# Hashed attention into a gated feed-forward: score and value matmuls in groups of six key tiles instead of three, and bit masks as second tensors

## Chip, cores and metric

The kernel runs on one core of a Trainium2 chip. The metric is device time in microseconds (us), the median of the runs shown, lower is better. A profile is one execution, recorded instruction by instruction; its times are from the start of its span.

## What is computed

Attention over 4 batches, 8 heads, 768 positions and a head width of 64, in which a query sees only the keys of its own hash bucket; then two matrix products with x * sigmoid(1.702 x) between.

```python
q_bits = (np.einsum('bhsd,dk->bhsk', q, proj) > 0).astype(np.int64)
k_bits = (np.einsum('bhsd,dk->bhsk', k, proj) > 0).astype(np.int64)
q_bucket = np.sum(q_bits * powers, axis=-1)          # six bits
k_bucket = np.sum(k_bits * powers, axis=-1)
mask = q_bucket[:, :, :, None] == k_bucket[:, :, None, :]
scores = np.where(mask, scale * np.matmul(q, k.transpose(0, 1, 3, 2)), -1000000000.0)
attn = np.exp(scores - np.max(scores, axis=-1, keepdims=True))
attn = attn / (np.sum(attn, axis=-1, keepdims=True) + 1e-09)
x = np.matmul(attn, v)                               # (B,H,S,D) -> (B*S, H*D) = 3072 x 512
h = x @ w_in                                         # 512 x 2048
return (h * (1.0 / (1.0 + np.exp(-1.702 * h)))) @ w_out
```

The weights arrive as float64 and are turned into float32 on the chip, by operations on their bits.

## The kernel before

**Stages.** Attention fills the first 345 us and leaves its result, transposed, in `xT`. The feed-forward stage (from line 632 on) does both products with seven block products in place of eight. It is not touched by the change but for its share of the weight conversion.

**Pairs, halves and groups.** The attention loop goes over 16 pairs of heads. The two heads of a pair lie on the two halves of the 128 partitions. Each pair has two halves c of its 384 queries, and six key tiles of 128. The loop before works in groups of three key tiles (GT = 3), so a pair is four groups. For a group:

- `scores` (L368, L369): for each key tile two matmuls of bf16 hash features, which add a large negative number where the buckets differ, and the float32 scores, as two 64-row matmuls side by side, into one of three PSUM buffers (`sps`, two banks each). ScalarE takes the exponential of a buffer into the tile `es[c]`; there is one `es` for each half.
- `add`: the sum over key tiles, for the denominators. GpSimd adds the first three tiles (L378, L379) into `acc0`, of which there is one buffer. VectorE adds the other three and `acc0` (L382 to L384).
- `values` (L392): matmuls of the exponentials with v, which accumulate all six tiles into `av`.
- `unload` (L403, L404): ScalarE copies `av` to `xT`.
- `total` (L410): the denominators as a matmul `dn` of the sum with ones. `invert` (L417, L419): VectorE transposes `dn` out of PSUM and takes the reciprocal. `norm` (L424, L425): VectorE transposes back and multiplies `xT`.

**The next pair** is prepared meanwhile: `turn` (L329, VectorE transposes k and q), `measure` (L336, ScalarE, sums of squares), `hashed` (L346, matmuls `hash`), `featured` (L351 on VectorE, then eight DMAs, L356, on the SP queue), `fetch` and `fetch_v` (DMAs of k, q and v, L291 and L298, on SP).

**PSUM.** The eight banks are taken: six by the three score buffers, one by `av`, one by the pool `mps`, of one buffer, in which `dn` of every half and `hash` of every pair take turns.

**Weight conversion** (`convert`, from L141). One chunk of 128 x 512 numbers for each of the pairs 1 to 14, in steps that `step` calls between other work: the DMA of `raw`; sign and bits (L155, L156); exclusive or (L158); a mask (L161) and, on ScalarE, the square for a size test (L163); a multiply of the low words (L165); an add (L167); and a multiply by the size test (L170). The remaining 18 chunks are converted in the feed-forward stage.

**Order.** TensorE, VectorE, ScalarE and GpSimd take their instructions in the order in which the program writes them (`manual_schedule`). A scheduler places only the DMAs of the SP queue. So an instruction that waits holds all that is written behind it on its engine. At group g the loop writes: scores of g; invert of a half finished earlier; turn and measure; norm; add, values and unload for group g - 1; hashed, featured and fetches; total of the half that ended at g - 3; conversion steps.

Of the kernel before, what the change touches and what calls it, by code (L numbers as in the profile page):

```python
# [8 lines left out]
F32 = mybir.dt.float32  # L9
# [10 lines left out]
P = 128  # L20
# [18 lines left out]
def kernel(  # L39
# [98 lines left out]

    CW = 512

    def convert(cv, dst, src, queue=nc.sync):  # L141

        raw = cv.tile([P, CW, 2], U32, tag="raw", name="raw")
        queue.dma_start(out=raw, in_=src)

        def of(x):
            return x if len(dst.shape) == 2 else x.rearrange("p (j d) -> p j d", j=dst.shape[1])

        lo, hi = raw[:, :, 0], raw[:, :, 1]
# [5 lines left out]
        nc.vector.tensor_scalar(sign, hi, 0x80000000, 0x40000000, op0=Alu.bitwise_and, op1=Alu.bitwise_or)  # L155
        nc.vector.tensor_scalar(bits, hi, 3, 0x7FFFFFFF, op0=Alu.logical_shift_left, op1=Alu.bitwise_and)  # L156
        yield
        nc.vector.tensor_tensor(bits, bits, sign, op=Alu.bitwise_xor)  # L158
        yield

        nc.vector.tensor_scalar(sign, bits, 0xFF800000, None, op0=Alu.bitwise_and)  # L161

        nc.scalar.activation(size, hi.bitcast(F32), Act.Square)  # L163
# [90 lines left out]
    def attention(ff):  # L254
# [4 lines left out]
        with actx:  # L259
# [99 lines left out]
            def scores(n, c, kts):  # L359
                qT, kT, qf, kf = xts[n, "q"], xts[n, "k"], feats[n % 2]["q"], feats[n % 2]["k"]  # L360
                cols = slice(c * HS, (c + 1) * HS)
                for kt in kts:
                    ps = sps.tile([P, 2, 512], F32, tag="s", name="ps")
                    keys = slice(kt * P, (kt + 1) * P)
                    for a, m, last in ((kf, qf, False), (kT, qT, True)):
                        for j in range(2):
                            hs = slice(D * j, D * (j + 1))
                            nc.tensor.matmul(ps[:, j, 0:HS], a[hs, keys], m[hs, cols], start=not last, stop=last)  # L368
                    nc.scalar.activation(es[c][:, kt, :, 0:HS], ps[:, :, 0:HS], Act.Exp, scale=1.0 / D**0.5)  # L369

            accs, avs = {}, {}

            def add(n, c, kt):

                e = [es[c][:, kt + i, :, 0:HS] for i in range(3)]
                if kt == 0:
                    acc = accs[n, c, 0] = st.tile([P, 2, HS], F32, tag="acc0", name="acc0", bufs=1)
                    nc.gpsimd.tensor_tensor(acc, e[0], e[1], op=Alu.add)  # L378
                    nc.gpsimd.tensor_tensor(acc, acc, e[2], op=Alu.add)  # L379
                else:  # L380
                    acc = accs[n, c] = st.tile([P, 2, HS], F32, tag="acc", name="acc")
                    nc.vector.scalar_tensor_tensor(acc, e[0], T * TINY, e[1], op0=Alu.add, op1=Alu.add)  # L382
                    nc.vector.tensor_tensor(acc, acc, e[2], op=Alu.add)  # L383
                    nc.vector.tensor_tensor(acc, acc, accs.pop((n, c, 0)), op=Alu.add)  # L384

            def values(n, c, kt):
                if kt == 0:
                    avs[n, c] = aps.tile([P, HS + 1], F32, tag="av", name="av")
                av, vt = avs[n, c], vts[n]
                for t in range(kt, kt + GT):  # L390
                    for j in range(2):
                        nc.tensor.matmul(av[D * j : D * (j + 1), :], vt[:, t, j, :], es[c][:, t, j, :],  # L392
                                         start=(t == 0), stop=(t == T - 1))
# [6 lines left out]
            def unload(n, c):  # L400
                av = avs.pop((n, c))
                vs = st.tile([P, 1], F32, tag="vs", name="vs")
                nc.scalar.copy(vs, av[:, HS : HS + 1])  # L403
                nc.scalar.activation(x_of(n, c), av[:, 0:HS], Act.Identity, bias=vs[:, 0:1])  # L404
# [7 lines left out]
            def invert(n, c):  # L412


                dn = accs.pop((n, c))
                rt = st.tile([P, HS], F32, tag="rt", name="rt", bufs=1)
                nc.vector.transpose(rt, dn)  # L417
                r = st.tile([P, HS // 32, 1], F32, tag="r", name="r")
                nc.vector.reciprocal(r, rt.rearrange("p (s i) -> p s i", i=32)[:, :, 0:1])  # L419
                accs[n, c] = rt, r  # L420

            def norm(n, c):
                rt, r = accs.pop((n, c))
                nc.vector.transpose(rt.rearrange("p (s i) -> p s i", i=32), r.to_broadcast([P, HS // 32, 32]))  # L424
                nc.vector.tensor_tensor(x_of(n, c), x_of(n, c), rt, op=Alu.mult)  # L425

            groups = [(n, c, kt) for n in range(len(pairs)) for c in range(2) for kt in range(0, T, GT)]
            last = len(pairs) - 1
            conv = {}

            def step(n, count=1):
                for _ in range(count):
                    next(conv.get(n, iter(())), None)
# [18 lines left out]
            started = {}  # L452
            first_pair()
            fetch_v(0)
            for x in "kq":
                fetch(1, x)
            for g in range(len(groups) + 4):
                n, c, kt = groups[g] if g < len(groups) else (last + 1, 0, 0)
                at = 2 * c + kt // GT
                if n <= last:  # L460
                    scores(n, c, range(kt, kt + GT))

                turns = at - (n == 0)
                if g in started:
                    invert(*started[g])
                if n < last and 0 <= turns < 2:
                    turn(n + 1, "kq"[turns])
                    measure(n + 1, "kq"[turns])
                if g in started:
                    norm(*started.pop(g))  # L470
                if 1 <= g <= len(groups):
                    add(*groups[g - 1])
                    values(*groups[g - 1])
                    if groups[g - 1][2]:
                        unload(*groups[g - 1][:2])
                if n < last and turns == 1:
                    hashed(n + 1)
                    featured(n + 1)
                    for x in "kq":
                        if n + 2 <= last:  # L480
                            fetch(n + 2, x)
                    fetch_v(n + 1)
                if 3 <= g <= len(groups) + 2 and groups[g - 3][2]:
                    total(*groups[g - 3][:2])
                    started[g + 1] = groups[g - 3][:2]
                if n == last and at in (1, 3):
                    guard(at // 2)
                if at == 0:
                    step(n)
                elif at == 1 and n > last - len(x_sums):  # L490
                    x_sums[n - last - 1]()
                elif at == 2:
                    step(n, 2)
                elif at == 3:
                    step(n, 4)
                    begin(n + 1)
                if g == len(groups):
                    for f in in_sums(0):
                        f()
                    invert(*started[g + 1])  # L500
                    norm(*started.pop(g + 1))
                    early.close()
                    next(ff)


    def shifted_attention():
# [273 lines left out]
```

## Time and profile before

| | us |
|---|---|
| median of 3 runs (936.3 to 937.06) | 936.75 |
| the profiled execution | 937.19 |
| its span, first to last instruction | 935.4 |
| mean granted TensorE clock | 0.996 of full speed |
| attention, to the first product of the feed-forward stage | 345.4 |
| one pair of heads in the steady part (from 168.1 to 188.7) | 20.6 |

A page of a profile gives the busy time of each engine and the chain of work that ended last. Rows of a group say: line, engine, operation, what is written and read, shape, count, then busy time, mean ns of one, and idle time before with what ended it. The timeline gives start, duration, engine, line and operation; overlapping matmuls are merged to one row with a count, so that the starts of rows, not their lengths, tell what TensorE spends. "PE" is TensorE, "DVE" VectorE, "ACT" ScalarE, "POOL" GpSimd, "SP" the queue of DMAs.

### The profile page before, as it was taken

The page shows a single profiled execution, that of the slowest core. Times are in us where ns is not written, and L with a number is a line of the kernel's source. Part 1 is how long each engine was busy: PE and PEld are TensorE (multiplying, and loading weights), DVE is VectorE, ACT ScalarE, POOL GpSimd, SP SyncE. Part 2 cuts the span into 40 slices and gives each one's busy share as a digit, 9 for nine tenths or more (in the row PEclk, how much of TensorE's full clock was granted, in tenths as well). Part 3 has the DMA queues.
Part 4 walks back from the last instruction along what each step waited for, and adds up shares of the span by engine and source line. Part 5 has one row for each costly group of instructions (what it writes and reads, how often), then busy time and mean ns, then how long its engine had stood idle before and what let it go on. Part 6 is the DMA issues. An engine that isn't in the chain of part 4 may idle for free.

```text
span 935.4 us, 11429 instructions
## 1 busy us (share of the span) xinstructions
PE 915.0 (98%) x4205; PEld 529.6 (57%) x4205; DVE 567.0 (61%) x786; ACT 301.8 (32%) x482; POOL 159.4 (17%) x124
## 2 busy tenths in 40 slices
PE   6899999999999999999999999999999999999995
PEld 3344444444444444444444444448888888888884
DVE  4489998899899965777777787334413232232310
ACT  4566666666666642322333232221000000000000
POOL 3224323322332370410010001300000000000000
PEclk9999999999999999999999999999999999999998
DMA  6344454443345102333333573236333333220001
GB/s 111 64 83 83 87 105 93 93 81 79 79 82 100 46 23 90 133 126 124 141 129 135 166 273 111 82 129 231 113 113 113 113 110 114 87 94 21 26 12 37
DMA packets 175331, 94.25 MB, mean 101 GB/s; under 512 B 126720, under 2 KB 158880, under 8 KB 175264
## 3 DMA queue, kind: packets, MB, share of 16 engines
q1 hardware_dynamic: 173392, 92.49, 34.9%
q10 hardware_dynamic: 1872, 0.92, 0.4%
q8 instruction: 35, 0.57, 0.3%
q14 instruction: 32, 0.26, 0.1%
HBM read 60.82 MB, written 31.46 MB: 99 GB/s over the span
## 4 chain that ended last, share of the span: by engine, by line
PE 96%; DMA 1%; DVE 1%; SPq 1%; issue 0%; ACTq 0%; ACT 0%; DVEq 0%
PE product L674 31%; PE product L632 31%; PE ps L368 16%; PE av L392 14%; PE dn L410 2%; PE hash L346 1%; DMA q<-in_q_dram 1%; SPq L356 1%; PE hash L322 0%; DMA k<-in_k_dram 0%; DVE bits L156 0%; PE tp L315 0%; DVE qT L329 0%; DVE kT L329 0%; DVE acc L383 0%
## 5 line engine op out<-in xcount | busy, mean ns | idle before, releaser
L369 ACT ACTIVATE e<-ps 128x768 f32<-128x768 f32 x192 | 153.7, 813 | 93.2 <-PE ps L368 91.5
L368 PE MATMUL ps<-qT,kT 64*128 64x384 f32 x768 | 155.2, 482 | 0.0
L392 PE MATMUL av<-e,v 128*64 128x385 f32 x768 | 138.4, 495 | 0.0
L632 PE MATMUL product<-xT,w_in_sb 128*128 128x512 f32 x288 | 135.5, 593 | 0.0
L636 ACT ACTIVATE c<-c 128x512 f32<-128x512 f32 x72 | 45.4, 632 | 180.0 <-DVE c L607 126.5
L603 ACT COPY u<-product 128x512 f32<-128x512 f32 x30 | 17.3, 578 | 246.7 <-PE product L674 242.0
L392 PEld LDWEIGHTS av<-e,v 128*64 128x64 f32 x768 | 49.3, 136 | 80.6 <-issue 80.4
L632 PEld LDWEIGHTS product<-xT,w_in_sb 128*128 128x128 f32 x288 | 54.6, 190 | 69.1 <-issue 60.7
L378 POOL TENSOR_TENSOR acc<-e 128x768 f32<-128x768 f32 x32 | 54.0, 1687 | 217.3 <-DVE acc L384 201.0
L632 PE MATMUL product<-t_x,s_in 128*128 128x512 f32 x192 | 90.2, 592 | 0.0
L368 PEld LDWEIGHTS ps<-qT,kT 64*128 64x128 f32 x768 | 68.4, 188 | 29.0 <-issue 29.0
L604 DVE TENSOR_TENSOR v<-product,u 128x512 f32<-128x512 f32 x30 | 20.6, 687 | 85.2 <-PE product L674 72.3
L368 PE MATMUL ps<-qf,kf 64*128 64x384 bf16 x384 | 63.4, 326 | 2.0 <-DMA qf<-f 2.0
L674 PE MATMUL product<-t_out,xT 128*128 128x256 f32 x288 | 63.6, 379 | 0.0
L674 PE MATMUL product<-w_out_sb,xT 128*128 128x256 f32 x288 | 63.6, 379 | 0.0
L674 PE MATMUL product<-w_out_sb,w_in_sb 128*128 128x256 f32 x288 | 63.6, 379 | 0.0
L632 PEld LDWEIGHTS product<-t_x,s_in 128*128 128x128 f32 x192 | 36.5, 190 | 45.9 <-issue 45.4
L674 PEld LDWEIGHTS product<-w_out_sb,xT 128*128 128x128 f32 x288 | 54.7, 190 | 7.9 <-issue 0.5
L674 PEld LDWEIGHTS product<-t_out,xT 128*128 128x128 f32 x288 | 54.7, 190 | 7.4
L674 PEld LDWEIGHTS product<-w_out_sb,w_in_sb 128*128 128x128 f32 x288 | 54.7, 190 | 7.4
L379 POOL TENSOR_TENSOR acc<-acc,e 128x768 f32<-128x768 f32 x32 | 55.6, 1739 | 2.5
L607 DVE TENSOR_TENSOR c<-product,c 128x512 f32<-128x512 f32 x30 | 20.7, 691 | 53.6 <-PE product L674 37.3
(122 smaller groups left out, 1115.5 us busy)
## 6 DMA issues: line engine op xcount, KB each, us to landing
g_dram<-c SPq DMA_DIRECT2D x72, 256.0 KB
xT<-g_dram SPq DMA_DIRECT2D x12, 1024.0 KB
w_in_sb<-g_dram SPq DMA_DIRECT2D x12, 1024.0 KB
raw<-in_moe_w_out_dram SPq DMA_DIRECT2D x16, 512.0 KB
raw<-in_moe_w_in_dram SPq DMA_DIRECT2D x15, 512.0 KB
v<-in_v_dram SPq DMA_DIRECT2D x32, 192.0 KB
g_dram<-u SPq DMA_DIRECT2D x24, 256.0 KB
k<-in_k_dram SPq DMA_DIRECT2D x60, 96.0 KB
```

Of the source, the lines that this page charges most:

```text
L368: nc.tensor.matmul(ps[:, j, 0:HS], a[hs, keys], m[hs, cols], start=not last, stop=last)
L369: nc.scalar.activation(es[c][:, kt, :, 0:HS], ps[:, :, 0:HS], Act.Exp, scale=1.0 / D**0.5)
L378: nc.gpsimd.tensor_tensor(acc, e[0], e[1], op=Alu.add)
L379: nc.gpsimd.tensor_tensor(acc, acc, e[2], op=Alu.add)
L392: nc.tensor.matmul(av[D * j : D * (j + 1), :], vt[:, t, j, :], es[c][:, t, j, :], start=(t == 0), stop=(t == T - 1))
L410: nc.tensor.matmul(dn[D * j : D * (j + 1), :], ones, acc[:, j, :], start=True, stop=True)
L603: nc.scalar.copy(u, product(1))
L604: nc.vector.tensor_tensor(v, product(6), u, op=Alu.add)
L607: nc.vector.tensor_tensor(c22, p, c21, op=Alu.add)
L632: nc.tensor.matmul(ps, wq[LEFT[i]][:, kc, :], xq[RIGHT[i]][:, kc, :], start=(kc == 0), stop=(kc == K2 - 1))
L636: nc.scalar.activation(c, c, Act.Gelu_apprx_sigmoid)
L674: nc.tensor.matmul(ps[:, m, :], x[:, m * P : (m + 1) * P], wqs[RIGHT[i]][:, c, :], start=(c == 0), stop=(c == FC // 2 - 1))
```

## The change

From pair 1 on, a group is all six key tiles of a half. The first pair keeps groups of three. Within group g the order becomes: scores of the six tiles and, directly after, GpSimd's add of the first three of them (`add_low`); `featured` of a pair hashed in the group before; VectorE's adds of the previous half (`add_high`); norm of the half before that; turn and measure of both k and q (in the first half of a pair); the previous half's values of three tiles, its `total`, its values of the other three, its unload; `hashed` and the fetches; conversion steps, with `invert` between them. In the first half of a pair one step goes ahead of `invert` and one behind, in the second half three and three, of which the last has work for one instruction. In `convert`, three operations with two immediate masks or one take the mask from a 128 x 1 tensor, broadcast over 512 columns, as second input; three memsets fill these tensors at the start.

```diff
+    masks = {}
+    for x in (0x40000000, 0x7FFFFFFF, 0xFF800000):
+        m = const.tile([P, 1], U32, name=f"mask_{x:x}")
+        nc.vector.memset(m, x)
+        masks[x] = m.to_broadcast([P, CW])
...
-        nc.vector.tensor_scalar(sign, hi, 0x80000000, 0x40000000, op0=Alu.bitwise_and, op1=Alu.bitwise_or)
-        nc.vector.tensor_scalar(bits, hi, 3, 0x7FFFFFFF, op0=Alu.logical_shift_left, op1=Alu.bitwise_and)
+        nc.vector.scalar_tensor_tensor(sign, hi, 0x80000000, masks[0x40000000], op0=Alu.bitwise_and, op1=Alu.bitwise_or)
+        nc.vector.scalar_tensor_tensor(bits, hi, 3, masks[0x7FFFFFFF], op0=Alu.logical_shift_left, op1=Alu.bitwise_and)
...
-        nc.vector.tensor_scalar(sign, bits, 0xFF800000, None, op0=Alu.bitwise_and)
+        nc.vector.tensor_tensor(sign, bits, masks[0xFF800000], op=Alu.bitwise_and)
...
-            groups = [(n, c, kt) for n in range(len(pairs)) for c in range(2) for kt in range(0, T, GT)]
+            groups = [(n, c, kts) for n in range(len(pairs)) for c in range(2)
+                      for kts in ((range(GT), range(GT, T)) if n == 0 else (range(T),))]
...
-            for g in range(len(groups) + 4):
-                n, c, kt = groups[g] if g < len(groups) else (last + 1, 0, 0)
-                at = 2 * c + kt // GT
-                if n <= last:
-                    scores(n, c, range(kt, kt + GT))
-
-                turns = at - (n == 0)
-                if g in started:
-                    invert(*started[g])
-                if n < last and 0 <= turns < 2:
-                    turn(n + 1, "kq"[turns])
-                    measure(n + 1, "kq"[turns])
-                if g in started:
-                    norm(*started.pop(g))
-                if 1 <= g <= len(groups):
-                    add(*groups[g - 1])
-                    values(*groups[g - 1])
-                    if groups[g - 1][2]:
-                        unload(*groups[g - 1][:2])
-                if n < last and turns == 1:
-                    hashed(n + 1)
-                    featured(n + 1)
+            for g in range(len(groups) + 2):
+                n, c, kts = groups[g] if g < len(groups) else (last + 1, 0, ())
+                prev = groups[g - 1] if 1 <= g <= len(groups) else None
+                if kts:
+                    scores(n, c, kts)
+                    if kts[0] == 0:
+                        add_low(n, c)
+                if hashes:
+                    featured(hashes.pop())
+                ended = prev and prev[2][-1] == T - 1
+                if ended:
+                    add_high(*prev[:2])
+                    totals.append((g + (g == len(groups) or len(kts) == GT), prev[:2]))
+                while norms:
+                    norm(*norms.pop(0))
+
+                turned = ("", "k", "q", "")[g] if n == 0 else "kq" if c == 0 and n < last else ""
+                for x in turned:
+                    turn(n + 1, x)
+                    measure(n + 1, x)
+                if prev:
+                    values(*prev[:2], prev[2][:GT])
+                inverted = []
+                while totals and totals[0][0] == g:
+                    inverted.append(totals.pop(0)[1])
+                    total(*inverted[-1])
+                if prev:
+                    values(*prev[:2], prev[2][GT:])
+                if ended:
+                    unload(*prev[:2])
+                if "q" in turned:
+                    hashed(n + 1)
+                    hashes.append(n + 1)
                     for x in "kq":
                         if n + 2 <= last:
                             fetch(n + 2, x)
                     fetch_v(n + 1)
-                if 3 <= g <= len(groups) + 2 and groups[g - 3][2]:
-                    total(*groups[g - 3][:2])
-                    started[g + 1] = groups[g - 3][:2]
...
-                if at == 0:
-                    step(n)
...
-                elif at == 2:
-                    step(n, 2)
-                elif at == 3:
-                    step(n, 4)
-                    begin(n + 1)
+                if kts and kts[-1] == T - 1:
+                    step(n, 1 + 2 * c)
+                for x in inverted:
+                    invert(*x)
+                    norms.append(x)
+                if kts and kts[-1] == T - 1:
+                    step(n, 1 + 2 * c)
+                    if c == 0 and n > last - len(x_sums):
+                        x_sums[n - last - 1]()
+                    if c == 1:
+                        begin(n + 1)
```

`add` is split: `add_low` holds its two GpSimd adds, `add_high` its three VectorE operations, with unchanged operands. `values` takes a range of tiles. At the end, the largest of the measured sizes is found one group later and `total` of the last half is written after the first task of the feed-forward stage, as before.

More of the change, by code (lines that the diff above doesn't have):

```diff
@@ L371, in attention, with add_low, add_high, values @@
             accs, avs = {}, {}
[L373 to L387, printed above, removed]
+            def add_low(n, c):
+                acc = accs[n, c, 0] = st.tile([P, 2, HS], F32, tag="acc0", name="acc0", bufs=1)
+                nc.gpsimd.tensor_tensor(acc, es[c][:, 0, :, 0:HS], es[c][:, 1, :, 0:HS], op=Alu.add)
+                nc.gpsimd.tensor_tensor(acc, acc, es[c][:, 2, :, 0:HS], op=Alu.add)
+            def add_high(n, c):
+                e = [es[c][:, GT + i, :, 0:HS] for i in range(GT)]
+                acc = accs[n, c] = st.tile([P, 2, HS], F32, tag="acc", name="acc")
+                nc.vector.scalar_tensor_tensor(acc, e[0], T * TINY, e[1], op0=Alu.add, op1=Alu.add)
+                nc.vector.tensor_tensor(acc, acc, e[2], op=Alu.add)
+                nc.vector.tensor_tensor(acc, acc, accs.pop((n, c, 0)), op=Alu.add)
+            def values(n, c, kts):
+                if 0 in kts:
                     avs[n, c] = aps.tile([P, HS + 1], F32, tag="av", name="av")
                 av, vt = avs[n, c], vts[n]
-                for t in range(kt, kt + GT):
+                for t in kts:
                     for j in range(2):
@@ L450, in guard @@
                     nc.vector.tensor_reduce(largest[0:1, 0:1], row, axis=AX.X, op=Alu.max)
-            started = {}
+            totals, norms, hashes = [], [], []
             first_pair()
@@ L482, in attention @@
                     fetch_v(n + 1)
-                if 3 <= g <= len(groups) + 2 and groups[g - 3][2]:
-                    total(*groups[g - 3][:2])
-                    started[g + 1] = groups[g - 3][:2]
-                if n == last and at in (1, 3):
-                    guard(at // 2)
-                if at == 0:
-                    step(n)
-                elif at == 1 and n > last - len(x_sums):
-                    x_sums[n - last - 1]()
-                elif at == 2:
-                    step(n, 2)
-                elif at == 3:
-                    step(n, 4)
-                    begin(n + 1)
+                if kts and kts[-1] == T - 1:
[9 more added lines that the diff above has]
+                        begin(n + 1)
+                if g == len(groups) - 1:
+                    guard(0)
                 if g == len(groups):
+                    guard(1)
                     for f in in_sums(0):
                         f()
-                    invert(*started[g + 1])
-                    norm(*started.pop(g + 1))
                     early.close()
                     next(ff)
+            while norms:
+                norm(*norms.pop(0))
     def shifted_attention():
```

## The prediction

> **What bounds the kernel now.** I read the busy shares first, then the chain that ended last, then the timelines of one steady pair of heads, engine by engine. From the page, busy time and the chain by line:
>
> ```profile
> PE 915.0 (98%) x4205; PEld 529.6 (57%) x4205; DVE 567.0 (61%) x786; ACT 301.8 (32%) x482; POOL 159.4 (17%) x124
> ...
> PE 96%; DMA 1%; DVE 1%; SPq 1%; issue 0%; ACTq 0%; ACT 0%; DVEq 0%
> ```
>
> TensorE sets the end in both stages, so only two things can move the time: fewer TensorE us, or a new wait of TensorE. Its timeline in a steady pair (start us, us, operation):
>
> ```profile
> 173.44 0.81 PE L410 MATMUL dn<-acc,ones 128*64 128x384 f32 x4
> 174.18 0.34 PE L368 MATMUL ps<-qf,kf 64*128 64x384 bf16 x2
> ...
> 176.71 2.16 PE L392 MATMUL av<-e,v 128*64 128x385 f32 x12
> 178.80 0.34 PE L368 MATMUL ps<-qf,kf 64*128 64x384 bf16 x2
> ...
> 188.69 0.52 PE L346 MATMUL hash<-kT,pf_k 128*32 128x384 f32 x2
> ```
>
> Starts tell the cost. From 174.18 three score tiles take 2.53 to the first value matmul, six value pairs 2.09 back to scores. Without switches, a tile follows a tile after 0.81 and a value pair a pair after 0.32, so three and six would be 2.43 and 1.92: each round trip between the score shape (64*128) and the value shape (128*64) costs about 0.27. The step from values to dn (same shape) costs nothing: 171.44 to 173.44 is 2.00. A pair of heads, hash to hash (168.08 to 188.69, and 20.56 on average), has four round trips and no idle.
>
> VectorE is not free beside that (about 18 of 20.6 us), and GpSimd holds it up. VectorE, then GpSimd, near the end of attention:
>
> ```profile
> 328.94 0.58 DVE L424 STREAM_TRANSPOSE rt<-r 128x384 f32<-128x384 f32 x1
> 329.56 1.41 DVE L425 TENSOR_TENSOR xT<-xT,rt 128x384 f32<-128x384 f32 x1
> ```
>
> ```profile
> 328.88 1.68 POOL L379 TENSOR_TENSOR acc<-acc,e 128x768 f32<-128x768 f32 x1
> ```
>
> The multiply of norm (L425) takes 0.56 alone. Here, at 330.97, it ends 0.41 after GpSimd's add ends at 330.56: it waited for it. The transpose of one input ahead of it was not held. Conversion lines in a steady pair, and in the feed-forward stage with GpSimd idle:
>
> ```profile
> 173.36 1.65 DVE L161 TENSOR_SCALAR sign<-bits 128x512 uint32<-128x512 uint32 x1
> ```
>
> ```profile
> 407.38 0.42 DVE L155 TENSOR_SCALAR sign<-raw 128x512 uint32<-128x512 uint32 x1
> 407.71 0.42 DVE L156 TENSOR_SCALAR bits<-raw 128x512 uint32<-128x512 uint32 x1
> 408.17 0.69 DVE L158 TENSOR_TENSOR bits<-bits,sign 128x512 uint32<-128x512 uint32 x1
> ```
>
> ScalarE, where a half is unloaded:
>
> ```profile
> 173.65 0.16 ACT L403 COPY vs<-av 128x1 f32<-128x1 f32 x1 [1.21 <-PE av L392]
> 173.84 0.58 ACT L404 ACTIVATE xT<-av,vs 128x384 f32<-128x384 f32 x1
> 174.32 0.67 ACT L163 ACTIVATE size<-raw 128x512 f32<-128x512 f32 x1
> 175.21 2.43 ACT L369 ACTIVATE e<-ps 128x768 f32<-128x768 f32 x3 [0.22 <-PE ps L368]
> ```
>
> The size of the conversion is queued behind the unload, which waits for the last value matmul. Before, VectorE's use of it (L170) came at 178.40, when it had been done for 3.4 us.
>
> **What the skill says.** The Trainium skill, "TensorEngine Tiling (Array Packing)", Key Properties: a change of tiling mode drains TensorE. The trace agrees, with the 0.27 above. "SBUF — State Buffer", sections SBUF: two separate sides and Who interferes with whom: a VectorE operation in a two-port mode or with two SBUF inputs and a GpSimd operation lock each other out for a whole instruction. L161 and L425 agree. So a mask as second tensor leaves the lock in place. "VectorE: DVE Perf Modes", perf-mode tier table: fp32 tensor_scalar runs at 2x, tensor_tensor at 1x; 0.42 and 0.69 agree.
>
> **The change, part by part.** Sums are made against the profiled execution, 937.19 us (span 935.4 and 1.8 around it), which lies 0.44 above the median of 936.75.
>
> *Groups of six.* A half becomes six tiles (2.53 + 2.42 = 4.95), three value tiles 1.99, dn 0.64, three more and the switch back 2.02: 9.60, for 9.89 before. A pair with its hash (0.83) would take 20.03, 0.53 less. ScalarE keeps up: exps pace 0.81 with TensorE, and three score buffers remain.
>
> *Who is late next.* Hash and dn share one PSUM bank (the pool of one buffer), so hash waits for L417, VectorE's read of dn. Before, L417 stood early in its group. Now VectorE's order in the first half of pair n+1 is: L170 of the last conversion, three adds of the second half of pair n (L382 to L384), norm (L424, L425), turn of k and of q, sign, bits, L417. And L170 now waits for size, which stands on ScalarE behind the unload of (n,0), whose values end just where scores of (n+1,0) start. From that moment (zero), with the trace's own spacings:
> - vs starts at 0.12 (173.65 is 0.21 after dn's start, and scores follow values 0.10 later than dn does); size ends 1.34 after it (173.65 to 174.99), at 1.46.
> - L170 at 1.51; next start 0.61 later (178.40 to 179.01).
> - adds at 2.12; 1.05 + 1.06 + 0.96: end 5.19. dn needs acc at 6.94, so dn isn't late.
> - GpSimd's first add of the new half waits for that buffer: from 5.33 (0.14 later, as at 172.87) to 6.87 (1.54).
> - L424 at 5.11, L425 at 5.70, held to 6.87, ends 7.28: 1.0 lost.
> - turns at 7.20 and 8.10 (0.90 each), sign 9.00, bits 9.61 (0.61 apart), L417 10.22 to 10.79.
> - hash at 10.84. TensorE would be ready at 9.60.
>
> So TensorE stands 1.24 in each pair. Period: 10.84 + 0.83 + 9.60 = 21.27 for 20.56, +0.71. Behind hash on TensorE stand all scores of the second half, and f, the features and the rest follow. In the second half VectorE reaches L170 about 1.0 before size, so nothing there adds.
>
> *Masks.* Three memsets at 0.06 hide under VectorE's wait to 8.71. Sign, bits and the third mask run as L158/L165 do, 0.69 for 0.42: the trace has no such form with a broadcast mask, and I bound it by 0.42 below and 0.69 plus one GpSimd add (1.67) above; I take 0.69, since GpSimd's second add ends at about 8.8, just before sign (from 6.95, its 1.67, and some 0.2 that L425 takes of it). Two of the three are on the path above: 2 x 0.28 of the 10.84. In the feed-forward stage 18 conversions x 3 x 0.27 = 15 us go into VectorE's idle (16.4 of 23 us busy from 416 to 439); TensorE has no gap there even at 395 to 401, where GpSimd stretches a conversion to 6.6 us. If that cover were gone, it would cost up to 15.
>
> *Moved DMAs.* The eight feature DMAs (0.8 each on SP) now start a group later, behind fetches of k, q, v. K's fetch waits for turn k (8.2): four k 2.1, four q 2.1, two v 1.1, so SP is free at 13.5, and features (ready at 12.5) have four issued at 16.7. They land about 2.4 later (33.4 against 31.0 in the first pair), before the next scores at 21.3. raw waits for size (1.5), lands about 4 later (180.2 to 184.3), before sign at 9.0. Nothing.
>
> *Ends.* The first pair keeps groups of three. Its features go 0.14 later, behind q's fetch. In pair 1, dn of the first half falls into the DMA wait (31.4 to 33.4): -0.65; its extra 1.45 (33.4 to 55.4 is 22.0, with hash waiting for turns from 43.4) becomes 0.81 (hash behind dn's end and L417): -0.64; switches -0.56. Pair 15 has no hash: -0.56.
>
> *Sum.* Pairs 2 to 14: 13 x 0.71 = +9.3; pair 1 -1.85; pair 15 -0.56; start +0.14: +7.0. 937.2 + 7.0 = 944.2, or **943.8** against the median.
>
> **The rivals.**
> - *The hold is not there* (L425 gets in front of GpSimd's add, which would then start later): hash at 9.84, 13 x 1.0 less: 930.8, **faster** than before. For it: many L425 in the steady pairs run in 0.56, as GpSimd's add ends just then. Against: four at the end of attention were all held until the add ended. It decides when more than 0.54 of the 1.24 goes.
> - *No stall at all*: the L417 path is under 9.60 for another reason (size early): 13 x 1.24 less, 927.7. Against: the order on ScalarE and the shared bank. This is the gain that the switches offer.
> - *Sign is held too*: GpSimd's second add ends only 0.19 before sign starts. Later by some tenths, it holds sign and then bits' start; 0.5 per pair gives 950.
> - *Part of the stall only*: 0.5 less per pair, 937.
>
> **How the numbers follow.** A measurement tells 0.2% (1.9 us) from no change. Forecast 0.56 (own range 940 to 948, 0.3 per pair either way); hold absent 0.15; no stall 0.08; sign held 0.12; part 0.09. Faster 0.25 (the two fast cases and a little of part), same 0.08, slower 0.67. The range 930 to 949 leaves out no stall and the far end of sign held.
>
> **What would show it.** In the timeline of the changed kernel: hash preceded by about 1.2 us of TensorE idle, released by VectorE's transpose of dn, in pairs 2 to 14; L425's counterpart in the first half at about 1.6 for 0.56; L170's counterpart preceded by a wait for size; mask operations at 0.69; halves of 9.60 without that wait. Wrong if hash starts with no gap (then about 928), or if TensorE waits for exps, for acc or for features, of which I expect none.

## The result and the profile after

The changed kernel takes **939.72 us** (median of 6 runs, 939.05 to 940.62) against 936.44 us for the kernel before in the same session (6 runs, 936.18 to 937.06): ratio **1.0035**, 95% interval 1.0022 to 1.0048. It is slower, by 3.3 us, where 7 were forecast. Its profiled execution took 939.21 us with a span of 937.4, against 937.19 and 935.4 before. Line numbers below are those of the changed kernel, unless another is named.

Busy time, and the chain that ended last, from the page:

```profile
PE 906.5 (97%) x4205; PEld 536.1 (57%) x4205; DVE 596.0 (64%) x789; ACT 296.4 (32%) x482; POOL 159.6 (17%) x124
...
PE 82%; DVE 10%; issue 3%; ACT 2%; DMA 1%; SPq 0%; DVEq 0%; ACTq 0%
```

TensorE is 8.5 us less busy with the same 4205 matmuls, which fits the switches saved. VectorE is recorded 29 us busier. The multiply of norm alone has 27.8 more (L432, 47.6 for the 19.8 of L425 before), since it now waits beside GpSimd in both halves of a pair; the three masked operations have only 3.7 more in sum, since bits waits less. But the chain, which held 96% TensorE before, now runs through VectorE for 10% of the span. The view of waits names the place (engine and line, what it waited for; us in total, times, longest):

```profile
PE hash L353 <- DVE rt L424: 13.3, 14, 1.0
...
DVE w_in_sb L177 <- ACT size L170: 9.9, 11, 0.9
...
PE av L399 <- ACT xT L411: 0.9, 1, 0.9
```

The first is what is lost, once in each of the pairs 1 to 14; the second is where it begins. One steady pair, TensorE's timeline (start us, us, operation, and in brackets the idle time before it with its releaser):

```profile
177.85 0.34 PE L375 MATMUL ps<-qf,kf 64*128 64x384 bf16 x2
...
182.80 2.16 PE L399 MATMUL av<-e,v 128*64 128x385 f32 x12
184.79 0.82 PE L417 MATMUL dn<-acc,ones 128*64 128x384 f32 x4
185.44 2.11 PE L399 MATMUL av<-e,v 128*64 128x385 f32 x12
188.52 0.52 PE L353 MATMUL hash<-kT,pf_k 128*32 128x384 f32 x2 [0.97 <-DVE rt L424]
```

Scores to values to hash would be 9.6; hash comes 10.67 after the scores. The period, hash to hash, is 21.08 in every pair from the second on (20.56 before). VectorE in the same stretch, from the last step of a conversion to the read of dn:

```profile
179.33 0.69 DVE L177 SCALAR_TENSOR_TENSOR w_in_sb<-size,w_in_sb 128x512 f32<-128x512 f32 x1 [0.90 <-ACT size L170]
179.94 0.95 DVE L389 SCALAR_TENSOR_TENSOR acc<-e 128x768 f32<-128x768 f32 x1
...
183.47 1.58 DVE L432 TENSOR_TENSOR xT<-xT,rt 128x384 f32<-128x384 f32 x1
184.97 0.96 DVE L336 STREAM_TRANSPOSE kT<-k 128x768 f32<-128x768 f32 x1
185.86 0.93 DVE L336 STREAM_TRANSPOSE qT<-q 128x768 f32<-128x768 f32 x1
186.72 0.65 DVE L162 SCALAR_TENSOR_TENSOR sign<-raw,mask 128x512 uint32<-128x512 uint32 x1
187.29 0.68 DVE L163 SCALAR_TENSOR_TENSOR bits<-raw,mask_7fffffff 128x512 uint32<-128x512 uint32 x1
187.89 0.57 DVE L424 STREAM_TRANSPOSE rt<-dn 128x384 f32<-128x384 f32 x1
```

ScalarE, which gives it its start, and GpSimd, which holds L432:

```profile
177.96 0.16 ACT L410 COPY vs<-av 128x1 f32<-128x1 f32 x1 [3.86 <-PE av L399]
178.16 0.58 ACT L411 ACTIVATE xT<-av,vs 128x384 f32<-128x384 f32 x1
178.63 0.66 ACT L170 ACTIVATE size<-raw 128x512 f32<-128x512 f32 x1
```

```profile
183.09 1.54 POOL L383 TENSOR_TENSOR acc<-e 128x768 f32<-128x768 f32 x1 [7.42 <-DVE acc L391]
```

The reader sees the whole chain from values to hash without a gap: the unload begins when the last value matmul is done, size is third behind it, L177 stands 0.90 for size, five operations later L432 waits for GpSimd's add (1.58 for an operation of 0.56), and sign and bits lie ahead of the read of dn on which hash waits.

### The profile page after: what moved, and what is told of

It reads as the page before. It is cut to its first block, busy times and chain, and to the rows that moved or that the text cites. A ratio compares the mean times of both kernels' runs of the same rounds, so it can differ in the third digit from the quotient of the medians.

```text
span 937.4 us, 11387 instructions
## 1 busy us (share of the span) xinstructions
PE 906.5 (97%) x4205; PEld 536.1 (57%) x4205; DVE 596.0 (64%) x789; ACT 296.4 (32%) x482; POOL 159.6 (17%) x124
## 4 chain that ended last, share of the span: by engine, by line
PE 82%; DVE 10%; issue 3%; ACT 2%; DMA 1%; SPq 0%; DVEq 0%; ACTq 0%
PE product L696 31%; PE product L654 31%; PE ps L375 10%; PE av L399 8%; DVE acc L390 1%; DVE acc L391 1%; DVE qT L336 1%; PE hash L353 1%; PE dn L417 1%; DVE acc L389 1%; DVE w_in_sb L177 1%; ACT xT L411 1%; DVE bits L163 1%; DVE sign L162 1%; ACT size L170 1%
## 5 line engine op out<-in xcount | busy, mean ns | idle before, releaser
L376 ACT ACTIVATE e<-ps 128x768 f32<-128x768 f32 x192 | 148.7, 812 | 38.7 <-PE ps L375 37.9
L399 PEld LDWEIGHTS av<-e,v 128*64 128x64 f32 x768 | 52.2, 136 | 76.2 <-issue 74.7
L383 POOL TENSOR_TENSOR acc<-e 128x768 f32<-128x768 f32 x32 | 49.4, 1543 | 220.9 <-DVE acc L391 201.7
L384 POOL TENSOR_TENSOR acc<-acc,e 128x768 f32<-128x768 f32 x32 | 59.7, 1866 | 2.5
```

What stands on the lines that cost most here:

```text
L383: nc.gpsimd.tensor_tensor(acc, es[c][:, 0, :, 0:HS], es[c][:, 1, :, 0:HS], op=Alu.add)
L384: nc.gpsimd.tensor_tensor(acc, acc, es[c][:, 2, :, 0:HS], op=Alu.add)
```

## The experiments

The theory to test: the stall ahead of hash is made by this chain, and each link is worth what it shows. Each time stands beside runs of the kernel before on the same chip (936.65, 937.38 and 936.72 in the three sessions). Beside the times I use from each trace the hash periods, and two stretches of the span: up to the end of the last VectorE operation, and the tail after it.

**Size early.** Size is computed on ScalarE in the same step as sign and bits, a half of a pair sooner.

```diff
-    def convert(cv, dst, src, queue=nc.sync):
+    def convert(cv, dst, src, queue=nc.sync, early=False):
...
+        if early:
+            nc.scalar.activation(size, hi.bitcast(F32), Act.Square)
...
-        nc.scalar.activation(size, hi.bitcast(F32), Act.Square)
+        if not early:
+            nc.scalar.activation(size, hi.bitcast(F32), Act.Square)
...
-                    conv[n] = convert(cv, *in_chunks[n - 1], nc.sync if n > 1 else nc.scalar)
+                    conv[n] = convert(cv, *in_chunks[n - 1], nc.sync if n > 1 else nc.scalar, early=True)
```

> The changed kernel with the square for the size test (ScalarE) written one step earlier in the attention's conversions, so that it stands behind the unload of the first half's group and not behind that of the second. Theory (the hash matmul waits for VectorE's transpose of dn, and that chain begins with the size multiply, which waits for the square): the multiply starts about 0.5 us after the scores of a new pair and not 1.48, the idle time ahead of hash falls from 1.04 to about 0.1 in 13 pairs, 12 us less: about 927.5. Rival 1 (the masks cost it: VectorE has too much work): no change, 939 to 940. Rival 2 (hash waits only because VectorE is full, and the wait for size merely shows its spare time): the idle time stays at 0.8 or more, above 937.

Measured: **928.90**, ratio 0.9916 (0.9902 to 0.9929). The period is 20.10 with no idle ahead of hash: size does head the chain. The gain of the large groups comes out once the wait is gone. It lies 1.2 above the price of no stall (927.7). That this is so near is in part luck: the price has no term for the end of the program, which is 2.2 us shorter here than before (see the tail below), and against it the wait is back in the last two hash periods (20.97 each). There VectorE has one more thing to do ahead of the adds, a column sum of x:

```profile
283.50 1.22 DVE L201 TENSOR_TENSOR xT<-xT 128x1024 f32<-128x1024 f32 x1
```

In the changed kernel these sums cost nothing: in three of the 14 pairs they stand in the place of the 0.9 that L177 otherwise waits for size, and the periods there are 21.08 and 21.09 like the others. With the wait gone VectorE is full, and they show.

**Masks back.** Groups as changed, bit operations with immediate masks as before.

```diff
-        nc.vector.scalar_tensor_tensor(sign, hi, 0x80000000, masks[0x40000000], op0=Alu.bitwise_and, op1=Alu.bitwise_or)
-        nc.vector.scalar_tensor_tensor(bits, hi, 3, masks[0x7FFFFFFF], op0=Alu.logical_shift_left, op1=Alu.bitwise_and)
+        nc.vector.tensor_scalar(sign, hi, 0x80000000, 0x40000000, op0=Alu.bitwise_and, op1=Alu.bitwise_or)
+        nc.vector.tensor_scalar(bits, hi, 3, 0x7FFFFFFF, op0=Alu.logical_shift_left, op1=Alu.bitwise_and)
...
-        nc.vector.tensor_tensor(sign, bits, masks[0xFF800000], op=Alu.bitwise_and)
+        nc.vector.tensor_scalar(sign, bits, 0xFF800000, None, op0=Alu.bitwise_and)
```

> The changed kernel with the three mask operations as before, with immediates and one tensor; all else as changed. Theory: sign and bits lie on the path to hash and take 0.7 for 1.17 us together, so the idle time ahead of hash falls by 0.46 in 13 pairs, 6 us: about 933.7. Rival 1 (the masks are the loss): back to the full gain of the fewer switches, about 927. Rival 3 (GpSimd holds the one-tensor form longer than the mask form): no change or slower, 940 or more.

Measured: **933.05**, ratio 0.9957 (0.9943 to 0.9970). The period is 20.54, 0.54 less: two operations by 0.27. As a price of the masks on this path that is right. It also says that the groups alone are faster than before (by 3.6, of which 2.5 lie in the tail, see below), and the masks take more than that back.

**Masks alone.** The kernel before, its groups of three and its order kept, with the three masked forms.

```diff
-        nc.vector.tensor_scalar(sign, hi, 0x80000000, 0x40000000, op0=Alu.bitwise_and, op1=Alu.bitwise_or)
+        nc.vector.scalar_tensor_tensor(sign, hi, 0x80000000, masks[0x40000000], op0=Alu.bitwise_and, op1=Alu.bitwise_or)
...
```

> The kernel before with the masks alone. Theory: VectorE is off the path there, so 936.4 within 0.7. Rival 1 (the masks cost by themselves, in attention or in the feed-forward stage): 938 to 942.

Measured: **941.99**, ratio 1.0059 (1.0045 to 1.0073). A miss: the theory had them covered. The period is 21.13 in ten of the last twelve, for 20.56. No idle shows ahead of hash; TensorE is busy by the records. The timeline tells it:

```profile
190.26 0.84 PE L353 MATMUL hash<-kT,pf_k 128*32 128x384 f32 x4
190.86 0.84 PE L353 MATMUL hash<-qT,pf_q 128*32 128x384 f32 x4
191.63 0.34 PE L375 MATMUL ps<-qf,kf 64*128 64x384 bf16 x2
```

Before, the matmuls of k and q were interleaved (both from 188.7) and scores followed after 0.78; here q's start 0.60 after k's and scores follow after 1.37. VectorE and GpSimd before:

```profile
184.84 1.92 DVE L156 TENSOR_SCALAR bits<-raw 128x512 uint32<-128x512 uint32 x1
...
187.47 0.98 DVE L329 STREAM_TRANSPOSE qT<-q 128x768 f32<-128x768 f32 x1
```

```profile
184.72 1.74 POOL L379 TENSOR_TENSOR acc<-acc,e 128x768 f32<-128x768 f32 x1
```

And in this kernel:

```profile
186.29 0.74 DVE L162 SCALAR_TENSOR_TENSOR sign<-raw,mask 128x512 uint32<-128x512 uint32 x1 [1.50 <-DMA raw<-in_moe_w_in_dram]
186.95 2.17 DVE L163 SCALAR_TENSOR_TENSOR bits<-raw,mask_7fffffff 128x512 uint32<-128x512 uint32 x1
...
189.82 0.98 DVE L336 STREAM_TRANSPOSE qT<-q 128x768 f32<-128x768 f32 x1
```

```profile
186.56 2.01 POOL L386 TENSOR_TENSOR acc<-acc,e 128x768 f32<-128x768 f32 x1
```

Bits waits for GpSimd's second add, to 188.57, and ends at 189.12. It waited in the kernel before too (1.92, in the pair whose hash begins at 188.69), but there the add ended 0.26 sooner after GpSimd's first one began (3.37 against 3.63), and bits had 0.30 left to do behind it, not 0.55. So turn q, and with it q's part of hash, is 0.5 later. The cover that the theory counted on was about 0.2: before, turn q ended at 188.45 and hash began at 188.69. The forecast of the change didn't need this number, since the order of VectorE is another there; as a statement on the masks in the old order the theory was wrong.

**Steps behind.** In the first half sign and bits stand behind the read of dn, not ahead of it.

```diff
-                if kts and kts[-1] == T - 1:
-                    step(n, 1 + 2 * c)
+                if c and kts and kts[-1] == T - 1:
+                    step(n, 3)
                 for x in inverted:
                     invert(*x)
                     norms.append(x)
...
-                    step(n, 1 + 2 * c)
+                    step(n, 2 + c)
```

> The changed kernel with the conversion step of a pair's first half (sign and bits) written behind the transpose of dn and not ahead of it. Theory: the transpose comes 1.17 us earlier, hash finds it done, no idle time is left in 13 pairs: about 926.2; the wait for size stays at its 0.9. Rival 1: no change, 939 to 940. Rival 2 (the features then come too late, since the step now lies ahead of them): the gain is lost in front of the scores, 935 or more.

Measured: **928.95**, ratio 0.9912 (0.9899 to 0.9926), above the expectation by the same return of the wait in the last two periods (20.87 and 21.03); the others are 20.04. The wait for size, expected to stay at 0.9, is gone from the trace: with the step moved behind it and the shorter period, VectorE is busy until L177 begins. But L177 begins 1.5 after the scores as in the changed kernel. So the chain need not lose its head: a shorter one, 1.2 less ahead of the read of dn, is enough.

**Hash in a bank of its own.** Hash is written to a score buffer; the order of all engines is kept.

```diff
-                h = dots[n] = mps.tile([P, HS], F32, tag="m", name="hash")
+                h = dots[n] = sps.tile([P, 2, 512], F32, tag="s", name="hash")[:, 0, 0:HS]
```

> The changed kernel with the hash of the next pair written to one of the three score buffers in PSUM, not to the bank that it shares with dn; nothing else is moved. If TensorE stands before hash because VectorE has not yet read dn out of the shared bank, the 1.0 us ahead of hash goes (hash then needs only the two turns, which end 0.7 before values do), and the third score tile behind it must find f done with the buffer: periods of about 20.1, 927 to 930 in all. If the chain through VectorE delays TensorE at some other point as well (acc for dn, or f for the scores' buffer), the idle moves there and the time stays at 937 to 941. The last two or three pairs, where VectorE also adds the column sums of x, may keep some of the wait, as they did in the kernel with size early.

Measured: **929.84**, ratio 0.9925 (0.9911 to 0.9938), period 20.08, no idle ahead of hash. VectorE's chain is as long as in the changed kernel; what tied TensorE to its end was the shared bank. In the last two periods (21.2) the wait turns up where the expectation put it, at the score tile whose buffer VectorE must first free by reading hash out of it into the features `f`:

```profile
PE ps L375 <- DVE f L358: 3.0, 3, 1.0
```

**Turn k first.** In the first half turn k stands ahead of norm, turn q behind it.

```diff
+                turned = ("", "k", "q", "")[g] if n == 0 else "kq" if c == 0 and n < last else ""
+                for x in turned[:1]:
+                    turn(n + 1, x)
+                    measure(n + 1, x)
                 while norms:
                     norm(*norms.pop(0))
-                turned = ("", "k", "q", "")[g] if n == 0 else "kq" if c == 0 and n < last else ""
-                for x in turned:
+                for x in turned[1:]:
```

> The changed kernel with the turn of k put ahead of norm (transpose and multiply of the finished half) and the turn of q behind it, in the first half of each pair. The transpose of k is one input wide and is not held by GpSimd, so the 1.0 us that the multiply of norm waits for GpSimd's first add is filled with it. If the mask operations are locked out by GpSimd as well, sign now comes 0.9 earlier, inside GpSimd's second add, and waits for its end: only 0.2 to 0.4 per pair is won, 934 to 937. If they are not, the whole 0.9 per pair is won: 927 to 929.

Measured: **936.82**, ratio 0.9996 (0.9988 to 1.0004), period 20.86: 0.22 won. The hold of norm's multiply is filled (L432 takes 0.72), and sign pays instead, since it now meets GpSimd's second add:

```profile
185.55 1.28 DVE L162 SCALAR_TENSOR_TENSOR sign<-raw,mask 128x512 uint32<-128x512 uint32 x1
```

```profile
184.40 1.88 POOL L384 TENSOR_TENSOR acc<-acc,e 128x768 f32<-128x768 f32 x1
```

The add ends at 186.28, sign at 186.83, 0.55 later. So the masked form is held as the others are: the rival "sign is held too" has the right mechanism. In the changed kernel sign starts at 186.72, the add ends at 186.59: it was missed by 0.13.

**Size early and masks back.** Both edits above together.

> The changed kernel with both repairs of the first runs at once: size computed early on ScalarE, and the three bit operations with immediate masks as before the change. If TensorE alone paces the steady pair once the size is early, the masks are covered there and cost nothing: hash periods of 20.1 as with size early alone. Masks back then help only where VectorE is still late, in the two last hash periods of 20.97 with the column sums of x: up to 0.6 each, so 927 to 929 against 928.9 with size early alone. If the masks cost by themselves wherever they stand (5.3 us in the order of before, 6.7 in the order of the change), 922 to 924.

Measured: **926.11**, ratio 0.9882 (0.9866 to 0.9898), a little below the expectation. The period is 20.04 throughout, the last two among them: 0.9 less in each of these (0.6 expected) and 0.06 in the others. So what the masks cost depends on the cover: 6.7 us in the changed order, 5.3 in the order of before, 2.8 with size early (the first and the last are taken between sessions, whose medians of before differ by up to 0.7).

**All mended.** This one with the four column sums of x all in the last pair, and the last half's values in a score buffer.

```diff
-                    avs[n, c] = aps.tile([P, HS + 1], F32, tag="av", name="av")
+                    if (n, c) == (last, 1):
+                        avs[n, c] = sps.tile([P, 2, 512], F32, tag="s", name="av")[:, 0, 0 : HS + 1]
+                    else:
+                        avs[n, c] = aps.tile([P, HS + 1], F32, tag="av", name="av")
...
-                    if c == 0 and n > last - len(x_sums):
-                        x_sums[n - last - 1]()
+                    if n == last:
+                        for f in x_sums[:2] if c == 0 else x_sums[2:]:
+                            f()
```

> The kernel with size early and immediate masks, and two more repairs at the end of attention: the four column sums of x (1.22 us each on VectorE) all stand in the last pair, where no hash follows, not one in each of the last four; and the last half's values go to a score buffer, so that they don't wait 0.87 us for ScalarE to unload the one av bank. Theory: the last two hash periods become 20.1 like the others and the wait of 0.87 is gone: about 926.5, at most 1.0 to 2.0 below the kernel without these two. Rival: the two sums in the last pair hold norm and acc of that pair, or values then wait for exps, and it is no faster (928).

Measured: **926.07**, ratio 0.9883 (0.9868 to 0.9898): no faster than the kernel without them. The sums had become free already, and the wait of 0.87 ahead of the last values became one of 0.67 ahead of the first product, for the same line of ScalarE, the unload to xT. These two kernels, alike within the measurement, are the fastest of the study, 1.2% below before, of which 0.2% lies in the tail.

**The tail.** In the traces, the time from the end of the last VectorE operation to the end of the span was 9.5 us before and 7.3 after. That is 2.2 us which no part of the forecast has. SyncE's closing instructions, by the instruction records (starts over 1 us apart, counted from the last instruction). The third column is my count of the instructions in SyncE's program, those of a branch that isn't taken included; no trace shows it.

| kernel | SyncE instructions run | last 13 in the program begin at | pauses at (from the end): us | tail |
|---|---|---|---|---|
| before | 749 | 1231 | 18: 1.62, 14: 2.77, **12: 2.20** | 9.52 |
| masks alone | 749 | 1228 | 18: 1.79, 14: 2.66, **9: 1.72** | 9.15 |
| changed | 712 | 1191 | 18: 1.48, 14: 2.81 | 7.27 |
| changed, 18 transfers more | 730 | 1227 | 16: 1.55, 14: 2.69, **8: 1.90** | 9.13 |
| before, 2 transfers more | 751 | 1235 | 16: 1.94, 14: 2.74 | 7.65 |
| changed, 37 transfers more | 749 | 1265 | 21: 1.75, 14: 2.67 | 7.37 |

The first three rows, and the other variants of the changed kernel (712 instructions, tails of 7.0 to 7.8), made the theory; the last three test it. The changed order needs 40 fewer instructions of SyncE by this count; the trace has 37 fewer run, all waits. The edit in the three, with 18, 2 and 37 for N, on `pad`, a tile that nothing reads:

```diff
             def outputs(n):
                 gq = g_views(n)
+                for i in range(N if n == 0 else 0):
+                    nc.sync.dma_start(out=pad[0:1, i : i + 1], in_=ones[0:1, 0:1])
```

> The changed kernel with 18 more transfers of 4 bytes issued by SyncE in the feed-forward stage, while its queue is idle; they stand twice in the program (the second time in the branch that isn't taken), so the end of SyncE's program lies 36 instructions later. In the profiles, SyncE's closing instructions pause a third time, for 2.2 and 1.7 us, in the two kernels with SyncE's 749 instructions (before, and before with masks alone), just after an 8 KB transfer of an instruction queue begins; in the eight kernels with 712 there are two pauses. Counted in the program, the pause falls on instruction 1233 in both. Theory: it is a fetch of the next piece of the program, and what the change won at the very end comes only from SyncE's program having become 40 instructions shorter. With 36 back, instruction 1233 lies among the last 13 again: a third pause of 1.7 to 2.2 us, the time 941.4 to 941.9. Rival (the end is shorter for another reason): no third pause, 939.7.

> The kernel before with 2 such transfers, 4 instructions of SyncE's program: its last 13 instructions now begin at 1235, behind 1233. Theory: the third pause goes, 934.3 to 934.9 for 936.5, with nothing else changed. Rival: two more transfers change nothing, 936.5.

> Control: the changed kernel with 37 such transfers, twice as many as in the first, 74 instructions: the last 13 then begin at 1265, well past 1233. Theory: no third pause, the time of the changed kernel, 939.7 (939.2 to 940.3). If the transfers themselves cost time, it is slower than the one with 18.

Measured: the changed kernel with 18, **942.85** (ratio to before 1.0063, 1.0049 to 1.0078); before with 2, **934.76** (0.9976, 0.9967 to 0.9986); the changed kernel with 37, **950.85** (1.0149, 1.0133 to 1.0164). The third pause comes and goes as expected in all three. Before with 2 transfers more is 2.0 us faster than before, and nothing but the place of SyncE's last instructions has been won: in its profile the tail is 1.87 shorter and the rest of the span 0.57 longer. So every time above is set against a before that carries these 2 us, as masks alone does too. By the ratios, against before with 2 transfers more, size early is 0.6% faster, the two fastest kernels 0.9%. In the profile's queue shares from the end of VectorE's last operation on, the instruction queue shows one 8 KB packet more where the pause is. This fits a fetch of the next piece of the program, which is argued from the packet; the runs show only that the pause goes with the place. Before, then before with 2 transfers more:

```profile
q14 instruction: 5, 0.04, 1.6%
```

```profile
q14 instruction: 4, 0.03, 1.2%
```

With 37 the time itself went wrong, and it is not the transfers as such. They depend on nothing, and the scheduler put them not at the feed-forward stage but where SyncE's queue first had room, 26 in a row ahead of a fetch of k:

```profile
35.14 15.36 SPq L691 DMA_DIRECT2D pad<-ones  x26
50.62 2.04 SPq L299 DMA_DIRECT2D k<-in_k_dram  x4
```

```profile
60.13 0.48 PE L376 MATMUL ps<-qf,kf 64*128 64x384 bf16 x1 [8.74 <-DMA qf<-f]
```

K came 11 us late (50.62 for 39.24 in the changed kernel), the features behind it too, and one period is 32.1 for 21.1. The run with 18 pays 1.1 in the same place (22.2), which fits its lying 0.95 above 941.9. As a control of the time the 37 are therefore void; as a control of the pause they hold. They also show what a full SyncE queue costs.

## Why the prediction was wrong in size

Direction and mechanism were as forecast; the size was not. By stretches of the profiled execution, from scores to scores (pair 1 begins at 33.42 before and 32.45 after, pair 2 at 55.42 and 51.38, pair 15 at 322.69 and 325.44, the first product at 345.39 and 349.78):

| stretch | forecast | measured |
|---|---|---|
| start | +0.14 | -0.97 |
| pair 1 | -1.85 | -3.07 |
| pairs 2 to 14 | +9.3 | +6.79 |
| pair 15 | -0.56 | +1.64 |
| feed-forward, to the last VectorE operation | 0 | -0.11 |
| tail | 0 | -2.25 |
| sum | +7.0 | +2.03 |

Of the 5.0 between the two sums, 2.5 lie in pairs 2 to 14 and 2.25 in the tail. The misses in the other four rows are as large (-1.1, -1.2, +2.2 and -0.1) and cancel to 0.2, which is luck.

- **Chain, order and place: right.** Unload, size, L177, adds, norm held by GpSimd, turns, sign, bits, read of dn, hash: each at the place given, and hash at 10.67 after the scores for a forecast of 10.84. Size early, steps behind and hash in its own bank each remove the stall by another link. The saving by fewer switches was right too: without the wait the period is 20.04 (size early and masks back), for a forecast of 20.03.
- **The stall of 1.24: mis-sized, the first failing term.** It is 1.07 (10.67 less 9.60; the view of waits has 0.97 of it as idle). The gaps between VectorE's starts were each taken from one pair of rows: 1.05 from the first add to the second (0.98 here), 0.90 per turn (0.89, 0.86), 0.61 from sign to bits (0.57). With hash to scores at 0.78 for 0.83, the period is 21.08 for 21.27. Small errors of one sign, times 13: 2.5 us.
- **The tail: not in the forecast at all, the second failing term.** 2.25 in the profile. The edit of before by 4 instructions gives 2.0 with nothing else changed. Against a before with its closing instructions on the same side, the changed kernel would be slower by some 5 (939.72 less 934.76).
- **Pair 1 and pair 15.** With groups of six, values lag by a half and no longer by a group, so three value tiles (1.0 us) go from the first pair to the last. I had left out both, and they cancel each other. The end also has the wait of 0.87 for the single av bank, which the forecast missed; another bank alone didn't win it back (all mended).
- **Start.** Earlier by 1.0, but the first hash of the shape of the steady pairs lies anywhere from 24.4 to 26.1 in the 13 traces, with no relation to the edits. It is no effect of the change that I can show.
- **Medians.** They differ by 3.3 and the profiled executions by 2.0: that of before lies 0.75 above the median given with the result, that of after 0.51 below.
- **Hold of L432: right** (1.58 forecast, 1.58 measured), though the lines it rested on were misread. Of the last four L425 before, three were held (1.41, 1.09, 1.08) and not four, and only the first beside GpSimd's add, the others beside its work for the feed-forward stage. Of the L425 in the steady pairs that ran in 0.56, one in two began as GpSimd's add ended (176.41, the add at 176.55), and beside the other GpSimd stood idle. The Trainium skill, "SBUF — State Buffer", Who interferes with whom, has the exclusive lock between GpSimd and VectorE operations with two SBUF inputs. The traces here agree, and a mask broadcast from one column counts as such an input by them: sign took 1.28 in the kernel with turn k first and bits 2.17 in masks alone, for 0.69 with GpSimd idle.
- **Masks: 0.69 each, right** for sign and bits (0.65 and 0.68); the third is held beside GpSimd in attention, 2.17 for 1.65 before, in the second half, behind which VectorE still waits 0.90 for size. They are hidden in the feed-forward stage, right: from 400 to 600 us VectorE is busy 162.6 for 147.5 before, and TensorE 200.0 of 200 in both.
- **Moved DMAs at nothing: right** as far as it went; no wait for features in a steady pair.
- **Rivals.** The hold was there, the stall was there, and sign was missed by 0.13. Closest is "part of the stall only" (937), though it asked for 0.5 per pair where 0.19 went; the rest of the way was the tail.

## What to carry to other kernels

When a change regroups the work of the bounding engine, follow the other engines' order to the next place where it waits for a shared buffer, and price that chain link by link. Here one small ScalarE operation queued behind an unload turned a gain of 0.6% into a loss of 0.6% (both without the tail's part), and moving it by one step gave the gain. What an operation costs is decided by the cover at its place: measure the cover (0.2 us here) before calling it hidden, and multiply the error of a period by its count before giving a range. Before a difference of 2 us is put down to the kernel's work, compare the tails: they can change with the length of a program alone.

## What was not expected of the hardware

- The end of a program can cost 1.7 to 2.2 us more or less, as the last instructions of SyncE fall on one side or the other of one place in its program (instruction 1233 by my count, in all three kernels with the pause); an 8 KB packet on an instruction queue goes with it. Which engine's fetch that packet is, the trace doesn't say.
- TensorE can lose 0.6 us in each pair with no idle in its records: matmuls of k and q of one shape (128*32), which otherwise run interleaved, run one after the other when the input of q is late (hash to scores 1.37 for 0.78).
- VectorE's transposes beside GpSimd's adds were not held (0.96 and 0.93 in each pair), while two-input operations beside them were, up to 2.17 for 0.69, and so was the one-input form of bits before (1.92 for 0.42). Held two-input operations ended 0.41 to 0.55 after the add, the one-input form 0.30 after it.
